# First row stage of a spectral filter and token-mixing kernel: row norms in pairs, the fold ahead of its small copy, a new order of loads and of VectorE and ScalarE

## The chip, the core and the metric

The kernel runs on one core of one Trainium2 chip. The time is the device time of one execution in microseconds (us). Of the kernel before, three executions are at hand besides a profiled one.

A core has TensorE (PE in the profile; its weight loads are PEld), VectorE (DVE), ScalarE (ACT), GpSimd (POOL) and SyncE (SP), which here only issues DMAs. Each engine works through its own instructions in the order in which they were written. What crosses from one engine to another is guarded by semaphores.

## The reference, cut to what matters

```python
def _A_ref(x, w_r, w_i):                       # spectral filter over tokens and channels
    X = jnp.fft.rfft2(x, axes=(-2, -1)) * (w_r + 1j * w_i)
    return jnp.fft.irfft2(X, s=(S, D), axes=(-2, -1))
def _B_ref(x, w1, b1, w2, b2):                 # token-mixing MLP, with its own layernorm
    u = _gelu(jnp.einsum("bsd,sf->bdf", _layernorm(x), w1) + b1)
    return (jnp.einsum("bdf,fs->bds", u, w2) + b2).transpose(0, 2, 1)
x = x + _A_ref(_layernorm(x), A_w_r, A_w_i)
x = x + _B_ref(_layernorm(x), B_w1, B_b1, B_w2, B_b2)
x = x + _A_ref(_layernorm(x), A_w_r, A_w_i)
x = x + _B_ref(_layernorm(x), B_w1, B_b1, B_w2, B_b2)
```

S is 2048, D 640, all in float32. The change concerns the first lines of this: the layernorm of the input x and the first step of the first Fourier transform.

## The kernel before

The 2048 tokens are laid out as 16 tiles of 128 partitions, called rows here (NJ is 16); a row is 128x640. The program is a sequence: the first row stage (in `run`), then for each of two rounds the column stage `a1` (the transforms over tokens, the filter and back), `a2` (back to channels, sum, second layernorm) and the MLP. The second round has its own row stage, which the change leaves as it is but for one load.

The first row stage takes each row i through these steps, each named here as its output is named in the profile:

- SP loads the row (`xt`) and, one per turn, a slab of the filter (`w`); at turns 4, 8 and 12 a quarter of the table of cosines and sines (`tM`), which serves four rows. Quarter 0 is loaded at the start, between row 1 and row 2.
- VectorE takes the row's statistics: two instructions for the halves (`st`, `stats1`), their aggregate (`mv`, `stats2`), and variance plus epsilon (`v`).
- GpSimd raises `v` to the power -0.5 (`r`; `mh` holds -0.5) and makes the offset `nb`, minus mean times r.
- ScalarE writes the normalized row (`z`), alternately into two buffers.
- GpSimd folds z (`eo`): two instructions on 128x320 each, the sum and the difference of mirrored halves (`a0_fold0`). VectorE copies two single columns of z into `eo` ahead of that (the small copy); GpSimd's fold waits for it.
- VectorE makes the rest, `fr`: two additions on 128x64 and a copy of two columns (`a0_rest`).
- TensorE multiplies `eo` and `fr` by the table and by its negative, which ScalarE writes (`tM<-tM`), after one filling matmul (`a0_s1f`). A filling matmul multiplies constants (`fill`); 28 stand ahead of row 0.
- ScalarE writes the result in half precision (`s1h`), VectorE what that leaves out (`s1l`).

Beside this ScalarE squares the filter's slabs (`jw`, into `xq`), whose largest sum sets a scale, `sx`. That takes two small products on TensorE with VectorE steps around them (`scale_x`, a generator whose steps are taken one by one): a product of `xq` with a unit matrix `eye`, a maximum (`xm`, `xb`), a product of `xb` with `eye`, then arithmetic on 128x16. `scale_b` does the like for a bias (`bsq`, `sqb`, `qb`).

The order of the work is that of the loop over i in `run`, turns 0 to 20 (NJ + 5): in turn i an engine works on different rows, the statistics of row i, the norm of row i-1, z of row i-2, fold, `fr` and matmuls of row i-3, `s1h` of row i-4, `s1l` of row i-5. Since `self.pin` is set, each engine keeps the order in which the loop writes its instructions.

The column stage follows. Its `dstage(g)` reads `s1h` and `s1l` of all rows at once (the profile's `tD,s1h`); four matmuls on `tD` stand ahead of it to keep TensorE busy. Part of `s1h` and `s1l` goes through memory and back, in another shape (`rest`, `stk`). The order in there is written by hand in `STEPS`: `d1@1` is dstage(1) into PSUM slot 1, `sA0@2` the first half of the next transform, and an entry that starts with e takes a step of one of the scale generators (`scale`: with a number above 7, of `scale_x`).

Buffers that matter: `eo` has three, `fr`, `r`, `nb`, `v`, `mv` and `st` two each, rows of x six, `w` four.

Of the kernel before, what the change touches and what calls it, by code (L numbers as in the profile page):

```python
# [11 lines left out]
F32 = mybir.dt.float32  # L12
# [3 lines left out]
AF = mybir.ActivationFunctionType  # L16
# [12 lines left out]
STEPS = '''  # L29
    d1@1 sA0@2 ph1 pl1 sB0 d2@3 sA1@0 d3@1 ph2&1 tb0 ta0 pl2 sa0 ph3 sB1 sb0 sA2@2 d4@3  # L30
    tb1 xh0&2 pl3 sB2 sA3@1 ta1 ph4&3 tb2 ta2 xl0 d6@0 sa1 sb1 ph6 sB3 xh1 d5@2 pl4 sa2 ta3 pl6 sb2 sA4@3 ph5 tb3 ul0&4
# [61 lines left out]
class Layers:  # L93
# [170 lines left out]
    def scale_x(self, pool, ps):  # L264
# [7 lines left out]
        V.tensor_copy(b, m.to_broadcast([NG, 128]))  # L272
        yield
        mm(ps[:, 1, 322:322 + NG], b, self.eye[:NG, :NG], start=True, stop=True)
        yield
# [74 lines left out]
    def a0_load(self, *parts):  # L350
        A = self.A
        todo = [(self.tD, A["tD"]), (self.tS2, A["tS2"]), (self.tI2, A["tI2"]), (self.tS1, A["tS1"])]
        for k in parts or range(4):
            self.nc.sync.dma_start(*todo[k])
            if parts == (3,):
                self.nc.sync.dma_start(self.tM32, A["tM32"][:, NJ - 1])

# [53 lines left out]
    def a0_fold0(self, z):  # L411

        G, V = self.G, self.V
# [8 lines left out]
    def a0_rest(self, eo):  # L422
# [93 lines left out]
    def a1(self, first):  # L516
# [1509 lines left out]
    def run(self):  # L2026
# [12 lines left out]
        order = list(range(NW, NG)) + list(range(NW))  # L2039
        x, st, eo, fr, pv, rb = ({} for _ in range(6))  # L2040
# [12 lines left out]
        load(0)  # L2053
        load(1)
        table(0)
        load(2)
        self.pin = True
        for i in range(NJ + 5):
            has = [0 <= i - k < NJ for k in range(6)]
            load(i + 3)  # L2060
            if i in (4, 8, 12):
                table(i // 4)
            for _ in range(2 if i == 5 else 1):
                if i >= 2 and order:
                    scans.append(self.scan_x(pw, order.pop(0)))
# [9 lines left out]
            if has[1]:  # L2075
                v, mv = st.pop(i - 1)
                r = self.t(self.pT, [128, 1], F32, "r", 2)
                self.G.tensor_tensor(r, v, self.mh, op=ALU.pow)
                b = self.t(self.pT, [128, 1], F32, "nb", 2)
                self.G.tensor_scalar(b, mv[:, 0:1], r, -1.0, op0=ALU.mult, op1=ALU.mult)  # L2080
                rb[i - 1] = r, b
            if has[2]:
                r, b = rb.pop(i - 2)
                self.T.activation(z[i % 2][:, :D], x.pop(i - 2), AF.Identity, scale=r, bias=b)
            if i % 4 == 2 and i < NJ:
                q = self.tM[i // 4]
                self.T.activation(q[:, 1], q[:, 0], AF.Copy, scale=-1.0)
            for _ in range(2 if i == 7 else 1):
# [4 lines left out]
            if i == 14:  # L2093
                gb = self.scale_b(at=lambda: px[:, 1, 400:401])
            if i in (14, 15):
                next(gb)
            if has[0]:
                s1 = self.stats1(self.pT, x[i])
                mv = self.stats2(self.pT, s1)
                v = self.t(self.pT, [128, 1], F32, "v", 2)  # L2100
                self.V.tensor_scalar(v, mv[:, 1:2], EPS, None, op0=ALU.add)
                st[i] = v, mv
            if i == NJ + 3:
                next(self.gx)
            if has[5]:
                self.a0_s1l(i - 5, pv.pop(i - 5), 1.0)
            if i == NJ + 2:
# [4 lines left out]
            if has[3]:  # L2112
                fr = self.a0_rest(eo[i - 3])
                pv[i - 3] = self.a0_s1f(i - 3, eo.pop(i - 3), fr)
            if i == NJ + 3:
                next(self.gx)
                next(gb)
        next(self.gx)
        next(gb)
# [223 lines left out]
```

## Time and profile before

| | us |
|---|---|
| median of three executions | 949.59 |
| lowest and highest of them | 948.35, 950.39 |
| the profiled execution's own time | 948.38 |
| its span in the trace | 946.6 |
| TensorE busy in the span | 932.1 (98%) |
| VectorE busy | 753.9 (80%) |
| ScalarE busy | 569.0 (60%) |
| GpSimd busy | 296.8 (31%) |

In the first row stage the shares are others. Of 10 us between 20 and 30 us, VectorE is busy 9.27, ScalarE 9.64, GpSimd 9.53 and TensorE 9.33 (its filling matmuls counted).

How to read the rows of a timeline: start in us from the span's start, duration in us, engine, line of the program, operation, output<-input, shapes, count; in square brackets the idle time ahead of it and what ended it. Rows of one kind that follow each other are merged, so the duration of an x2 is that of both. Instructions of one engine overlap a little: from one start to the next is what an instruction costs the queue. Line 85 is a helper through which all engine calls pass, so instructions are told apart by their tiles. A row of waits gives who waited for whom, the time in all, how often, and the longest. A row of groups gives the busy time in us and the mean in ns behind the bar.

### The profile page before, as it was taken

Reading aid. Unit: us, or ns where it says so; the run is one execution under the profiler, and the core shown is the slowest. Engines: PE = TensorE matmul, PEld = TensorE weight load, DVE = VectorE, ACT = ScalarE, POOL = GpSimd, SP = SyncE. Lnnn points to the kernel's source line nnn. Section 1 sums busy time; section 2 is a strip of 40 time slices with the busy share of each in tenths; the row PEclk is TensorE's granted clock in tenths of the full one; section 3 lists DMA queues with packets and bytes.
Section 4 is the critical chain, followed back from the end, with each engine's and each line's share of the span. In section 5 each row is a group of like instructions: output and inputs, shape, how many; then the busy total and the mean of one; then the engine's idle time right before and its main releaser. Section 6 shows DMA issues by size and latency. Waiting matters only on the chain.

```text
span 946.6 us, 22342 instructions
## 1 busy us (share of the span) xinstructions
PE 932.1 (98%) x8996; PEld 685.5 (72%) x8996; DVE 753.9 (80%) x1411; ACT 569.0 (60%) x861; POOL 296.8 (31%) x453
## 2 busy tenths in 40 slices
PE   8999999999999999999999999999999999999998
PEld 5677777767777777777777777777777777777776
DVE  6869999999788978777775898889745446998885
ACT  5948789885676755555552576783433335465542
POOL 6949688111111033322223695770000000000000
PEclk9999999999999999999999999999999999999999
DMA  8945367555776856855342746774455446665411
GB/s 282 323 127 172 117 225 237 204 178 204 289 265 234 292 179 220 281 177 173 118 136 81 204 137 204 256 238 160 157 159 167 142 126 239 198 190 183 137 55 49
DMA packets 68816, 177.84 MB, mean 188 GB/s; under 512 B 7756, under 2 KB 16232, under 8 KB 68712
## 3 DMA queue, kind: packets, MB, share of 16 engines
q1 hardware_dynamic: 62040, 152.30, 49.6%
q0 software_dynamic: 6672, 24.12, 6.7%
q8 instruction: 70, 1.15, 0.5%
q14 instruction: 34, 0.28, 0.1%
HBM read 128.81 MB, written 47.58 MB: 186 GB/s over the span
## 4 chain that ended last, share of the span: by engine, by line
PE 81%; DVE 9%; POOL 3%; ACT 3%; DMA 2%; issue 2%; SPq 0%; DVEq 0%; ACTq 0%; POOLq 0%
PE ps L85 81%; DVE st L85 2%; DMA xt<-x 1%; POOL xl L85 1%; DVE s1l L85 1%; DMA raw<-w 1%; POOL ta L85 1%; DVE xt L85 1%; POOL eo L85 1%; DVE hl L85 1%; DVE hf L85 1%; DVE hlb L85 1%; DVE fr L85 1%; POOL xt L85 0%; ACT eh L85 0%
## 5 line engine op out<-in xcount | busy, mean ns | idle before, releaser
L85 PEld LDWEIGHTS <-wh 128*128 128x128 f16 x2290 | 221.9, 98 | 85.9 <-ACT wh L85 0.4
L85 PE MATMUL ps<-u,wh 128*128 128x320 f16 x1234 | 227.2, 299 | 0.0
L85 PEld LDWEIGHTS <-wl 128*128 128x128 f16 x1617 | 157.8, 98 | 62.5 <-issue 1.2
L85 PE MATMUL ps<-u,wl 128*128 128x320 f16 x817 | 180.7, 299 | 0.0
L85 PEld LDWEIGHTS <-wo 128*128 128x128 f16 x917 | 89.6, 98 | 34.8
L85 POOL TENSOR_TENSOR r<-v,mh 128x1 f32<-128x1 f32 x64 | 38.2, 596 | 119.7 <-DVE nm L85 113.0
L85 PE MATMUL ps<-tDi,Yh 128*128 128x322 f16 x320 | 70.0, 300 | 0.9 <-ACT Yh L85 0.8
L85 ACT ACTIVATE junk<-raw 128x896 bf16<-128x896 f32 (+1 forms) x60 | 59.5, 992 | 10.3 <-DMA raw<-w 9.6
L85 DVE SCALAR_TENSOR_TENSOR wl<-raw,s,wh 128x896 f16<-128x896 f32 (+2 forms) x43 | 56.3, 1317 | 11.3 <-ACT wh L85 11.3
L85 POOL TENSOR_TENSOR eo<-z 128x320 f32<-128x320 f32 x60 | 57.8, 983 | 21.4 <-ACT z L85 14.8
L85 POOL TENSOR_TENSOR xt<-xt,ec 128x320 f32<-128x320 f32 x64 | 53.2, 853 | 29.2 <-DVE xt L85 29.1
L85 DVE BATCH_NORM_STATS2 st<-xt 128x6 f32<-128x320 f32 x126 | 55.5, 482 | 4.9 <-DMA xt<-x 4.1
L85 PE MATMUL ps<-u,wo 128*128 128x320 f16 x413 | 57.9, 299 | 0.0
L85 PE MATMUL ps<-tDi,Yl 128*128 128x322 f16 x192 | 54.2, 299 | 0.1
L85 ACT ACTIVATE wh<-raw,s 128x896 f16<-128x896 f32 (+2 forms) x46 | 45.1, 988 | 6.5 <-PE ps L85 6.5
L85 POOL TENSOR_TENSOR xl<-ta,xh 128x642 f16<-128x642 f32 (+2 forms) x34 | 45.7, 1347 | 4.7 <-ACT xh L85 4.5
L85 DVE SCALAR_TENSOR_TENSOR u<-f,su,u 128x1280 f16<-128x1280 f32 (+2 forms) x26 | 25.5, 997 | 25.2 <-ACT u L85 25.1
L85 PE MATMUL ps<-hhb,wh 128*128 128x320 f16 x256 | 43.4, 299 | 0.0
L85 ACT ACTIVATE z<-xt,nb,r 128x640 f32<-128x640 f32 x31 | 28.5, 918 | 24.0 <-POOL z L85 15.7
L85 PE MATMUL ps<-tD,s1h 128*64 128x160 f16 (+1 forms) x576 | 39.2, 236 | 0.8 <-ACT s1h L85 0.5
L85 PEld LDWEIGHTS <-Yh 128*128 128x128 f16 x320 | 28.7, 97 | 14.4 <-ACT Yh L85 1.2
L85 DVE SCALAR_TENSOR_TENSOR f<-ps,cp,f 128x320 f32<-128x320 f32 x41 | 22.4, 545 | 19.7 <-PE ps L85 19.7
(267 smaller groups left out, 2199.0 us busy)
## 6 DMA issues: line engine op xcount, KB each, us to landing
xt<-x SPq DMA_DIRECT2D x79, 320.0 KB, 3.0
raw<-w SPq DMA_DIRECT2D x32, 512.0 KB, 7.1
x<-xt SPq DMA_DIRECT2D x47, 320.0 KB, 2.8
raw<-w SPq DMA_DIRECT2D x32, 448.0 KB, 4.9
raw<-w2z SPq DMA_DIRECT2D x32, 448.0 KB, 4.0
w<-w SPq DMA_DIRECT2D x43, 321.0 KB, 4.6
out<-xt SPq DMA_DIRECT2D x15, 320.0 KB, 2.2
w1S<-wl POOLq DMA_DIRECT2D x9, 512.0 KB, 6.6
```

The costliest lines, as they stand in the source:

```text
L85: i = f(*a, **k)
```

## The change

1. *Norms in pairs.* Rows 0 and 1 keep a norm each. From row 2 on two rows share one: the aggregates go side by side into one tile, `v` and a new tile `nm` (minus the mean, on VectorE) are made for both rows by one instruction each in the turn of the second row, and GpSimd makes `r` and `nb` on 128x2. `nb` is now a product of two tensors, `nm` and `r`. These norms are taken in even turns, for rows i-2 and i-1, and stand on GpSimd ahead of the fold of row i-3.
2. *The small copy behind the fold.* The copy of two columns moves from `a0_fold0` to the head of `a0_rest`, behind the fold in the program's order; GpSimd's fold no longer waits for it.
3. *Loads.* Row 2 is loaded ahead of table quarter 0. The table in memory is cut into four pieces of 128x512, each contiguous; before, a quarter was 2 KB out of every 8 KB. The second load of slab `w` in turn 5 is gone; one is loaded per turn.
4. *Order.* `fr` and the matmuls of a row move one turn later (row i-4 in turn i), and `s1h` with them (row i-5). `s1h` now stands at the head of ScalarE's turn; z stands ahead of the filter's squaring in odd turns and turns below 5 and behind it in the others. VectorE's turn begins with the small copy and `fr`, then come the statistics, `s1l`, and only then the aggregate, `v` and `nm`. z has three buffers.
5. *Scales.* The product of `xq` with `eye` moves behind the last row's matmuls; that of `xb` into the column stage, ahead of dstage(1) (`ep9`), and the arithmetic on 128x16 behind it (`ev9`). `bsq` is squared in turn 13 instead of 14 and reduced in turn 15.
6. *Filling.* 20 filling matmuls ahead of row 0 instead of 28, and two on `tD` instead of four ahead of dstage(0).

On VectorE, in the middle of the stage, one turn before, from the statistics of row 7:

```order
L85 BN_STATS st_453<-xt_327 128x6 x2
L85 BN_AGGR mv_456<-st_453 128x2
L85 TENSOR_SCALAR v_458<-mv_456 128x1
L85 SCALAR_TENSOR_TENSOR s1l_195<-ps_393,s1h_194 128x160x4
L85 TENSOR_TENSOR fr_461<-eo_441 128x2x32
L85 TENSOR_TENSOR fr_461<-eo_441 128x64
L85 COPY fr_461<-eo_441 128x2
L85 COPY eo_481<-z_218 128x2
```

And now, the odd turn with the statistics of row 7 (`xt_289`), from its head to its end:

```order
L85 COPY eo_381<-z_217 128x2
L85 TENSOR_TENSOR fr_417<-eo_381 128x2x32
L85 TENSOR_TENSOR fr_417<-eo_381 128x64
L85 COPY fr_417<-eo_381 128x2
L85 BN_STATS st_429<-xt_289 128x6 x2
L85 SCALAR_TENSOR_TENSOR s1l_195<-ps_393,s1h_194 128x160x4
L85 BN_AGGR mv_404<-st_429 128x2
L85 TENSOR_SCALAR v_434<-mv_404 128x2
L85 TENSOR_SCALAR nm_436<-mv_404 128x2
```

`fr` has moved ahead of the statistics, `s1l` between the statistics and their aggregate, and `v` and `nm`, for rows 6 and 7 together, stand at the end; the even turn lacks these two.

On GpSimd, some rows in, before (`eo` is a fold, `r` and `nb` a norm):

```order
L85 TENSOR_TENSOR eo_370<-z_217 128x2x160 x2
L85 TENSOR_TENSOR r_374<-v_349,mh 128x1
L85 TENSOR_SCALAR nb_376<-mv_347,r_374 128x1
L85 TENSOR_TENSOR eo_405<-z_218 128x2x160 x2
L85 TENSOR_TENSOR r_409<-v_386,mh 128x1
L85 TENSOR_SCALAR nb_411<-mv_384,r_409 128x1
```

And now:

```order
L85 TENSOR_TENSOR eo_345<-z_219 128x2x160 x2
L85 TENSOR_TENSOR r_377<-v_368,mh 128x2
L85 TENSOR_TENSOR nb_379<-nm_370,r_377 128x2
L85 TENSOR_TENSOR eo_381<-z_217 128x2x160 x2
L85 TENSOR_TENSOR eo_411<-z_218 128x2x160 x2
L85 TENSOR_TENSOR r_447<-v_434,mh 128x2
L85 TENSOR_TENSOR nb_449<-nm_436,r_447 128x2
```

Instead of a norm after each fold there is one norm, twice as wide, after each two. The fold right behind the norm (`eo_381`, row 3) is the one that the odd turn of VectorE shown above begins with.

The diff, cut to its core:

```diff
@@ STEPS
-    d1@1 sA0@2 ph1 pl1 sB0 d2@3 ...
+    ep9 d1@1 ev9 sA0@2 ph1 pl1 sB0 d2@3 ...
@@ scale_x
     yield
+        ps = self.px
         mm(ps[:, 1, 322:322 + NG], b, self.eye[:NG, :NG], start=True, stop=True)
@@ a0_fold0
-        V.tensor_copy(eo[:, 0:162:161], z[:, 0:162:161])
         G.tensor_tensor(v2(eo, 1, 161), za, zb, op=ALU.add)
@@ a0_rest
+        V.tensor_copy(eo[:, 0:162:161], z[:, 0:162:161])
@@ a0_s1f
-        for _ in range(FILL if j else 28):
+        for _ in range(FILL if j else 20):
@@ a1
+        self.px = slots[3]
-            for _ in range(4):
+            for _ in range(2):
@@ run
-        z = [self.pT.tile([128, 642], F32, name=f"z{k}") for k in range(2)]
+        z = [self.pT.tile([128, 642], F32, name=f"z{k}") for k in range(3)]
-            nc.sync.dma_start(self.tM[q][:, 0], A["tM32"][:, 4 * q:4 * q + 4])
+            nc.sync.dma_start(self.tM[q][:, 0], A["tM32"][q].rearrange("p (a b) -> p a b", a=4))
+        def norms(k, n):
+            r = self.t(self.pT, [128, 2], F32, "r", 2)[:, :n]
+            self.G.tensor_tensor(r, vs[k], self.mh[:, 0:1].to_broadcast([128, n]), op=ALU.pow)
+            b = self.t(self.pT, [128, 2], F32, "nb", 2)[:, :n]
+            self.G.tensor_tensor(b, nms[k], r, op=ALU.mult)
+            for q in range(n):
+                rb[k + q] = r[:, q:q + 1], b[:, q:q + 1]
         load(0)
         load(1)
+        load(2)
         table(0)
-        load(2)
-            for _ in range(2 if i == 5 else 1):
-                if i >= 2 and order:
+            if i >= 2 and order:
+            if has[1] and i - 1 in one:
+                norms(i - 1, 1)
+            elif has[1] and i % 2 == 0:
+                norms(i - 2, 2)
             if has[3]:
-                eo[i - 3] = self.a0_fold0(z[(i - 3) % 2])
+                eo[i - 3] = self.a0_fold0(z[(i - 3) % 3])
+            if has[5]:
+                self.a0_s1h(i - 5, pv[i - 5], 1.0)
+            if i % 2 or i < 5:
+                norm()
...
+            if not i % 2 and i > 4:
+                norm()
             if has[4]:
-                self.a0_s1h(i - 4, pv[i - 4], 1.0)
+                fr = self.a0_rest(eo[i - 4], z[(i - 4) % 3])
+                pv[i - 4] = self.a0_s1f(i - 4, eo.pop(i - 4), fr)
             if has[0]:
                 s1 = self.stats1(self.pT, x[i])
-                mv = self.stats2(self.pT, s1)
...
             if has[5]:
                 self.a0_s1l(i - 5, pv.pop(i - 5), 1.0)
+            if has[0]:
+                k, n = (i, 1) if i in one else (i - i % 2, 2)
+                if k == i:
+                    mv = self.t(self.pT, [128, 2, 2], F32, "mv", 2)[:, :n]
+                self.V.bn_aggr(mv[:, i - k], s1)
+                if i - k == n - 1:
+                    vs[k] = self.t(self.pT, [128, 2], F32, "v", 2)[:, :n]
+                    self.V.tensor_scalar(vs[k], mv[:, :, 1], EPS, None, op0=ALU.add)
+                    nms[k] = self.t(self.pT, [128, 2], F32, "nm", 2)[:, :n]
+                    self.V.tensor_scalar(nms[k], mv[:, :, 0], -1.0, None, op0=ALU.mult)
@@ _shape_tables
-    t["tM32"] = (m1 * TS).astype(np.float32)
+    t["tM32"] = (m1 * TS).astype(np.float32).reshape(128, 4, 512).transpose(1, 0, 2)
```

`norm()` writes z of row i-2 and, in turns 3, 6, 10 and 14, the negative of a table quarter.

More of the change, by code (lines that the diff above doesn't have):

```diff
@@ L29 @@
 STEPS = '''
[L30 removed]
+    ep9 d1@1 ev9 sA0@2 ph1 pl1 sB0 d2@3 sA1@0 d3@1 ph2&1 tb0 ta0 pl2 sa0 ph3 sB1 sb0 sA2@2 d4@3
     tb1 xh0&2 pl3 sB2 sA3@1 ta1 ph4&3 tb2 ta2 xl0 d6@0 sa1 sb1 ph6 sB3 xh1 d5@2 pl4 sa2 ta3 pl6 sb2 sA4@3 ph5 tb3 ul0&4
@@ L355, in a0_load @@
             if parts == (3,):
-                self.nc.sync.dma_start(self.tM32, A["tM32"][:, NJ - 1])
+                self.nc.sync.dma_start(self.tM32, A["tM32"][3, :, 384:])
     CA, CB = 1.0 / ZS ** 2, EPS / ZS ** 2
@@ L411, in a0_fold0 @@
     def a0_fold0(self, z):
-        G, V = self.G, self.V
+        G = self.G
         eo = self.t(self.pT, [128, 646], F32, "eo", 3)
@@ L420, in a0_fold0, with a0_rest @@
         return eo
-    def a0_rest(self, eo):
+    def a0_rest(self, eo, z):
         V = self.V
@@ L2039, in run @@
         order = list(range(NW, NG)) + list(range(NW))
-        x, st, eo, fr, pv, rb = ({} for _ in range(6))
-        z = [self.pT.tile([128, 642], F32, name=f"z{k}") for k in range(2)]
+        x, eo, pv, rb, vs, nms = ({} for _ in range(6))
+        z = [self.pT.tile([128, 642], F32, name=f"z{k}") for k in range(3)]
         for q in z:
@@ L2050, in table @@
         def table(q):
-            nc.sync.dma_start(self.tM[q][:, 0], A["tM32"][:, 4 * q:4 * q + 4])
+            nc.sync.dma_start(self.tM[q][:, 0], A["tM32"][q].rearrange("p (a b) -> p a b", a=4))
[6 more added lines that the diff above has]
+                rb[k + q] = r[:, q:q + 1], b[:, q:q + 1]
         load(0)
         load(1)
+        load(2)
         table(0)
-        load(2)
         self.pin = True
+        one = 0, 1
         for i in range(NJ + 5):
@@ L2062, in run @@
                 table(i // 4)
-            for _ in range(2 if i == 5 else 1):
-                if i >= 2 and order:
-                    scans.append(self.scan_x(pw, order.pop(0)))
+            if i >= 2 and order:
+                scans.append(self.scan_x(pw, order.pop(0)))
             if i == 8:
@@ L2072, in run @@
                     self.a0_load()
+            if has[1] and i - 1 in one:
+                norms(i - 1, 1)
+            elif has[1] and i % 2 == 0:
+                norms(i - 2, 2)
             if has[3]:
-                eo[i - 3] = self.a0_fold0(z[(i - 3) % 2])
[L2075 to L2088, printed above, removed]
+                eo[i - 3] = self.a0_fold0(z[(i - 3) % 3])
+            if has[5]:
+                self.a0_s1h(i - 5, pv[i - 5], 1.0)
+            def norm():
+                if has[2]:
+                    r, b = rb.pop(i - 2)
+                    self.T.activation(z[(i - 2) % 3][:, :D], x.pop(i - 2), AF.Identity, scale=r, bias=b)
+                if i in (3, 6, 10, 14):
+                    q = self.tM[i // 4]
+                    self.T.activation(q[:, 1], q[:, 0], AF.Copy, scale=-1.0)
@@ L2089, in run @@
+            if i % 2 or i < 5:
+                norm()
+            for _ in range(2 if i == NJ + 2 else 1):
                 if i >= 4 and scans:
                     scans.pop(0)()
-            if has[4]:
-                self.a0_s1h(i - 4, pv[i - 4], 1.0)
[L2093 to L2096, printed above, removed]
+            if not i % 2 and i > 4:
+                norm()
+            if i == 13:
+                gb = self.scale_b(at=lambda: px[:, 1, 400:401])
@@ L2097, in run @@
+            if i in (13, 15):
+                next(gb)
+            if has[4]:
+                fr = self.a0_rest(eo[i - 4], z[(i - 4) % 3])
+                pv[i - 4] = self.a0_s1f(i - 4, eo.pop(i - 4), fr)
             if has[0]:
                 s1 = self.stats1(self.pT, x[i])
-                mv = self.stats2(self.pT, s1)
-                v = self.t(self.pT, [128, 1], F32, "v", 2)
-                self.V.tensor_scalar(v, mv[:, 1:2], EPS, None, op0=ALU.add)
-                st[i] = v, mv
             if i == NJ + 3:
-                next(self.gx)
@@ L2105, in run @@
-            if has[5]:
-                self.a0_s1l(i - 5, pv.pop(i - 5), 1.0)
-            if i == NJ + 2:
                 assert not scans
@@ L2111, in run @@
                 next(self.gx)
[L2112 to L2115, printed above, removed]
+            if i == NJ + 4:
                 next(self.gx)
                 next(gb)
-        next(self.gx)
+            if has[5]:
+                self.a0_s1l(i - 5, pv.pop(i - 5), 1.0)
+            if has[0]:
[8 more added lines that the diff above has]
+                    self.V.tensor_scalar(nms[k], mv[:, :, 0], -1.0, None, op0=ALU.mult)
         next(gb)
```

## The prediction

> **What bounds the kernel now.** I read the page first, for the span and the engine that carries the end.
>
> ```profile
> span 946.6 us, 22342 instructions
> PE 81%; DVE 9%; POOL 3%; ACT 3%; DMA 2%; issue 2%; SPq 0%; DVEq 0%; ACTq 0%; POOLq 0%
> ```
>
> PE carries four fifths of the chain. The change touches only the first row stage, the first 52 us, so I read that stage alone: its waits, then the timeline of VectorE and GpSimd. The steady part of the stage (14 to 44 us) repeats every 2.56 us. On VectorE one row is:
>
> ```profile
> 25.14 0.88 DVE L85 BATCH_NORM_STATS2 st<-xt 128x6 f32<-128x320 f32 x2
> 26.12 0.21 DVE L85 BATCH_NORM_AGGREGATE mv<-st 128x2 f32<-128x12 f32 x1
> 26.37 0.15 DVE L85 TENSOR_SCALAR v<-mv 128x1 f32<-128x1 f32 x1
> 26.44 0.81 DVE L85 SCALAR_TENSOR_TENSOR s1l<-ps,s1h 128x640 f16<-128x640 f32 x1
> 27.17 0.35 DVE L85 TENSOR_TENSOR fr<-eo 128x64 f32<-128x64 f32 x2
> 27.55 0.17 DVE L85 COPY fr<-eo 128x2 f32<-128x2 f32 x1
> 27.63 0.16 DVE L85 COPY eo<-z 128x2 f32<-128x2 f32 x1
> 27.70 0.88 DVE L85 BATCH_NORM_STATS2 st<-xt 128x6 f32<-128x320 f32 x2
> ```
>
> On GpSimd, the same stretch:
>
> ```profile
> 24.50 0.56 POOL L85 TENSOR_TENSOR r<-v,mh 128x1 f32<-128x1 f32 x1
> 25.15 0.27 POOL L85 TENSOR_SCALAR nb<-mv,r 128x1 f32<-128x1 f32 x1
> 25.38 1.72 POOL L85 TENSOR_TENSOR eo<-z 128x320 f32<-128x320 f32 x2
> 27.06 0.55 POOL L85 TENSOR_TENSOR r<-v,mh 128x1 f32<-128x1 f32 x1
> ```
>
> Each row of either engine starts where the one ahead of it lets go: both are full at 2.56 us (25.14 to 27.70, 24.50 to 27.06). TensorE has slack; in the waits of 14 to 44 us (total, times, longest) it stands for the folds, and VectorE once for ScalarE's bsq:
>
> ```profile
> PEld ps L85 <- POOL eo L85: 5.8, 11, 0.7
> ...
> DVE sqb L85 <- ACT bsq L85: 0.6, 1, 0.6
> ```
>
> So this stage is set by VectorE and GpSimd together, and a row gains only what both give up.
>
> At the head, the first fold waits behind the statistics of row 2, which wait for a DMA:
>
> ```profile
> 3.60 0.89 DVE L85 BATCH_NORM_STATS2 st<-xt 128x6 f32<-128x320 f32 x2 [1.87 <-DMA xt<-x]
> 4.77 0.15 DVE L85 TENSOR_SCALAR v<-mv 128x1 f32<-128x1 f32 x1
> 8.40 0.89 DVE L85 BATCH_NORM_STATS2 st<-xt 128x6 f32<-128x320 f32 x2 [2.26 <-DMA xt<-x]
> 9.71 0.16 DVE L85 COPY eo<-z 128x2 f32<-128x2 f32 x1
> ```
> ```profile
> 5.00 0.55 POOL L85 TENSOR_TENSOR r<-v,mh 128x1 f32<-128x1 f32 x1 [4.14 <-DVE v L85]
> 6.88 0.27 POOL L85 TENSOR_SCALAR nb<-mv,r 128x1 f32<-128x1 f32 x1
> 9.96 1.70 POOL L85 TENSOR_TENSOR eo<-z 128x320 f32<-128x320 f32 x2 [2.81 <-DVE eo L85]
> ```
> ```profile
> 5.95 0.92 ACT L85 ACTIVATE z<-xt,nb,r 128x640 f32<-128x640 f32 x1 [1.02 <-POOL nb L85]
> 7.46 0.63 ACT L85 ACTIVATE tM<-tM 128x512 f32<-128x512 f32 x1 [0.59 <-DMA tM<-tM]
> ```
>
> z of row 0 is done at 6.87 (5.95 + 0.92), the fold starts at 9.96: 3.1 us lie between.
>
> **The change, part by part.** I follow three marks: V5 and V15, the starts of v for rows 5 and 15, and E, the end of row 15's last matmul. Before, V5 is 15.97, V15 42.49, E 52.31 (51.93 + 0.38):
>
> ```profile
> 15.97 0.15 DVE L85 TENSOR_SCALAR v<-mv 128x1 f32<-128x1 f32 x1
> ...
> 42.49 0.15 DVE L85 TENSOR_SCALAR v<-mv 128x1 f32<-128x1 f32 x1
> ```
> ```profile
> 49.97 0.39 PE L85 MATMUL ps<-fill 128*128 128x512 f16 x1
> 50.20 1.89 PE L85 MATMUL ps<-tM,eo 128*128 128x256 f32 x8
> 51.93 0.38 PE L85 MATMUL ps<-tM,fr 128*128 128x128 f32 x2
> 52.24 0.39 PE L85 MATMUL ps<-eye,xb 16*128 16x16 f32 x2
> ...
> 52.60 1.02 PE L85 MATMUL ps<-tD 128*128 128x512 f16 x4
> 53.55 1.33 PE L85 MATMUL ps<-tD,s1h 128*64 128x160 f16 x32
> ```
> ```profile
> 52.35 0.70 ACT L85 ACTIVATE s1h<-ps 128x640 f16<-128x640 f32 x1 [1.90 <-PE ps L85]
> ```
>
> *Head.* x2 now stands ahead of the table in SP's queue. By windows of the DMA view, the stretches 0 to 3.8, 3.8 to 6.4 and 6.4 to 9 us moved:
>
> ```profile
> DMA packets 274, 0.64 MB, mean 169 GB/s; under 512 B 22, under 2 KB 22, under 8 KB 274
> DMA packets 192, 0.37 MB, mean 142 GB/s; under 512 B 25, under 2 KB 25, under 8 KB 192
> DMA packets 462, 1.05 MB, mean 404 GB/s; under 512 B 50, under 2 KB 50, under 8 KB 462
> ```
>
> The first 0.64 MB are x0 and x1 (0.33 each); then 2.6 us at 142 GB/s, just until the table lands (7.46, about 1 us behind its bytes); then full speed. I take the slow stretch to be the table, 2 KB pieces out of rows of 8 KB. x2 then follows x1 at full speed: bytes done at 4.6, landed at 5.6 instead of 8.4. If the table, now contiguous, runs at 400 GB/s too, x3 lands at 7.1; if it stays slow, at 9.0. Now by hand: nb of row 1 ends near 7.14 (before 6.88 + 0.27; one more VectorE instruction per row, 0.07, and a shorter nb on GpSimd), and the fold of row 0, which no longer waits for VectorE, runs 7.15 to 8.85. Rows 2 and 3 share one norm, which needs both: statistics at 6.22 and 7.45, v at 8.68, pow at 8.9. Then nb, and the fold of row 1 ends at 11.4 + d, where d is what a second column adds to pow. V5 follows 2.27 later (below): 13.7 + d. Gain 2.3 - d.
>
> *Two rows at a time.* Throughput alone would promise much: GpSimd loses half of 0.91 per row, and VectorE, with s1l between the statistics and their aggregate, loses the wait of 0.18 (0.98 to 0.80) and some of v: 2.56 to about 2.4. But the order makes a loop. GpSimd does the norm for rows i-2, i-1 ahead of the fold of row i-3; VectorE's next odd turn begins with the rest of that same row (its copy, fr), and its v comes at that turn's end. The loop is one for two rows: v to pow 0.23 (4.77 to 5.00), pow to nb 0.65 + d (24.50 to 25.15), nb 0.17, folds 1.68 (25.38 to 27.06), to fr 0.03 (a bare hand-over), fr and copy 0.47, statistics 0.80, s1l 0.73, aggregate to v 0.24. Sum 5.00 + d, against 5.12. nb is now a product of two tensors, as in the later rows:
>
> ```profile
> L85 POOL TENSOR_TENSOR nb<-nm,r 128x1 f32<-128x1 f32 x15 | 2.8, 189 | 1.2
> ```
>
> From its 0.189 to pow's 0.55 there are 0.36; if that is all per column, d is 0.36, if none, 0. I take the middle, 0.18, since no row has pow on two columns. Below 0 it can't be: two columns hold the work of one. The Trainium skill (GPSIMD Engine Reference, section 3.1) gives about 2.6 cycles per element for an ordinary two-input operation; by that d is about 0.002 us and the sum would be 4.4 rather than 3.2, but no run here shows that it holds for pow. Five loops, V5 to V15: 25.0 + 5d against 26.52 (which holds 0.6 of waiting for ScalarE's bsq, now issued two turns earlier). Gain 1.5 - 5d. The small copy now also stands behind a fold: hidden under the fold's second half if it waits for the first only; if for both, 0.08 per loop, 0.4 in all. I take it as hidden.
>
> *Tail.* Rows 12 to 15 end on TensorE. A row there takes 2.3 us: fill 0.23 (49.97 to 50.20), eo 1.73 to 1.83, fr 0.27. Row 12's start waits for its small copy (V15 + 0.25), row 13 ends near V15 + 4.8, row 15 at V15 + 9.4 + d/2, against 9.82 before. Gain 0.4 - d/2.
>
> *Behind E.* Before, E to the first s1h matmul is 1.24. Two warming matmuls fewer save 0.5 of it, but s1h of row 15 (0.70 on ScalarE) ends no earlier, so the first matmul starts at E + 0.85 or so. The xq product now stands behind E, under that wait; the xb product (about 0.2) moves behind the first s1h group, so 0.2 of the 0.35 is paid back: gain 0.2, bounds 0 and 0.4. The chain sx (four VectorE instructions) moves too, into VectorE's idle time there. Eight fills fewer cost nothing, since they only cover the wait for row 0. The third z buffer and its 0.1 us MEMSET lie in GpSimd's idle head.
>
> Sum: 2.3 - d + 1.5 - 5d + 0.4 - d/2 + 0.2 = 4.4 - 6.5d, at d = 0.18: 3.2 us. The profiled execution took 948.38 (span 946.6 and 1.8 around it) and would take 945.2; it is the fastest of three whose median is 949.59, so the median should go to 946.4. Behind E the order of work is the same but for the sx steps, so I expect the shift to arrive in full. The measurement can tell about 0.2%, 1.9 us.
>
> **Rivals.**
>
> 1. *The table stays slow* (the slow stretch is not its row pitch). x3 lands at 9.0, v of row 3 is at 10.27, V5 at 15.3 + d: head gain 0.7 - d, sum 2.8 - 6.5d = 1.6: 948.0. For it: no row says that the pitch is the cause; the first touch of a tensor could be slow too. Against it: x0, the first touch of its tensor, ran in the faster stretch.
>
> 2. *The two-row loop costs more than it saves: slower.* Place: norm, fold, fr, statistics, v, once in two rows. If pow on two columns costs two whole instructions (d = 0.55), the small copy waits for the whole fold (0.4), and the table stays slow, the sum is 2.8 - 3.6 - 0.4 = -1.2: 950.8. With the copy's 0.4 it turns negative from d = 0.37 on, or from 0.62 if the table is fast. For it: pow is the dearest one-column step of the stage (0.55 against 0.15 for v), and pairing puts the second row's norm ahead of an earlier row's fold. Against: the fixed cost is visible in nb's 0.189 for one column.
>
> 3. *TensorE's clock drops at the head.* Two queries of TensorE's timeline, to 9 and to 13 us, group the fills:
>
> ```profile
> 1.79 7.54 PE L85 MATMUL ps<-fill 128*128 128x512 f16 x22 [1.79 <-DVE fill L2034]
> ...
> 1.79 8.83 PE L85 MATMUL ps<-fill 128*128 128x512 f16 x28 [1.79 <-DVE fill L2034]
> ```
>
> The last six took 1.29, 0.215 each; for 22 to take 7.54, some 12 at the start took twice that, until about 7 us. Twenty fills end near 8.9; if row 0 starts at 10.5 (rival 1), TensorE idles 1.6 us. If that brings the early rate back for as long as it held at first (1.79 to 7, 5.2 us), half of that, 2.6, is lost: gain 0.6, 949.0. The trace holds no such gap behind the fills, so nothing in it speaks for the drop. The Trainium skill (TensorE: Matmul & The Clock Gate, Part 1) says that the clock halves after an idle window of about 3.4 us and comes back after a busy one; the trace agrees on the two rates, not on the time, and by that rule 1.6 us would not suffice.
>
> 4. *The gain is lost behind E*: the next stage waits for the transfers of s1h and s1l through memory or for VectorE, whatever E does. Then nothing arrives: 949.6. Against: those transfers start from row 15's s1l too.
>
> **How the numbers follow.** Forecast (table fast, d between 0 and 0.36) 0.52; rival 1 0.28; rival 2 0.09; rival 3 0.05; rival 4 0.06. The forecast's own gains run from 2.1 (d = 0.36) to 4.4, rival 1's from 0.5 to 2.8. The range goes from a gain of 4.4 and the executions' scatter of about 1 (944.2) to rival 1's worst with the copy in line and a little scatter (949.8). Faster by over 1.9 us: nine tenths of the forecast (0.47), two fifths of rival 1 (0.11), a little of rival 3 (0.02): 0.60. Slower: rival 2, whose worst lies beyond 1.1 only if scatter helps, taken whole as a caution, with what I overlook: 0.09. Within: 0.31.
>
> **What would show it.** In the profile after: the fold of row 0 starts near 7.15; statistics of row 2 near 6.2 and of row 3 near 7.5 (rival 1: 9.0); r on 128x2 lasts 0.73 (0.55 to 0.91); two rows take about 5.16 us, with VectorE waiting about 0.5 before each second fr for GpSimd's eo, and GpSimd about 0.5 for v; E near 49.2. The prediction is wrong if two rows take under 4.8 (the loop isn't there) or over 5.3, if x2 still lands near 8, or if E moves and the end doesn't.

## The result and the profile after

| | before | after |
|---|---|---|
| median, four executions each (us) | 949.08 | 956.08 |
| lowest and highest | 948.35, 950.39 | 955.30, 958.46 |
| the profiled execution's own time | 948.38 | 955.76 |
| its span | 946.6 | 954.0 |

After to before is 1.0082, with a 95% interval of 1.007 to 1.0094: slower by 7 us, where 3 us of gain were forecast. The time lies above the range, which ended at 949.8.

On the page of after, TensorE's share of the chain has gone from 81% to 80% and VectorE's from 9% to 11%:

```profile
PE 80%; DVE 11%; ACT 3%; issue 2%; DMA 2%; POOL 2%; SPq 0%; ACTq 0%; DVEq 0%; POOLq 0%
```

Nearly all of it, 6.8 of the 7.4 us by which the span grew, arises in the first row stage. The waits of after between 14 and 44 us (total, times, longest) show who stands there now:

```profile
POOL r L85 <- DVE nm L85: 11.0, 5, 2.2
PEld ps L85 <- DVE eo L85: 10.6, 9, 1.7
PE ps L85 <- DVE eo L85: 7.1, 9, 1.3
```

GpSimd, full before, now waits 2.2 us in every two rows for `nm`, and TensorE for VectorE's part of `eo`. The timeline of GpSimd in after, over two rows (x4 is two folds, one right behind the other):

```profile
15.87 0.76 POOL L85 TENSOR_TENSOR r<-v,mh 128x2 f32<-128x2 f32 x1 [2.20 <-DVE nm L85]
...
16.85 3.34 POOL L85 TENSOR_TENSOR eo<-z 128x320 f32<-128x320 f32 x4
22.39 0.74 POOL L85 TENSOR_TENSOR r<-v,mh 128x2 f32<-128x2 f32 x1 [2.20 <-DVE nm L85]
```

And that of VectorE in the same two rows:

```profile
15.77 0.16 DVE L85 COPY eo<-z 128x2 f32<-128x2 f32 x1
15.84 0.35 DVE L85 TENSOR_TENSOR fr<-eo 128x64 f32<-128x64 f32 x2
...
17.93 0.63 DVE L85 COPY eo<-z 128x2 f32<-128x2 f32 x1
18.58 1.70 DVE L85 TENSOR_TENSOR fr<-eo 128x64 f32<-128x64 f32 x2
```

Two rows take 6.52 us (15.87 to 22.39) and not 5.16. The same two `fr` instructions last 0.35 at 15.84, beside the norm, and 1.70 at 18.58, beside the second fold; the small copy 0.16 and 0.63. They are not shown as waiting: they have started and do not end. The second `fr` ends at 20.28, just behind the second fold (16.85 + 3.34 = 20.19). The difference of 1.35 (1.70 - 0.35) is the whole of what a pair lasts too long.

The head went as forecast, in the rows of VectorE and then of GpSimd:

```profile
6.31 0.88 DVE L85 BATCH_NORM_STATS2 st<-xt 128x6 f32<-128x320 f32 x2
...
7.86 0.89 DVE L85 BATCH_NORM_STATS2 st<-xt 128x6 f32<-128x320 f32 x2 [0.43 <-DMA xt<-x]
```
```profile
7.18 1.70 POOL L85 TENSOR_TENSOR eo<-z 128x320 f32<-128x320 f32 x2
9.35 0.75 POOL L85 TENSOR_TENSOR r<-v,mh 128x2 f32<-128x2 f32 x1 [0.47 <-DVE nm L85]
```

And the end of the stage on TensorE:

```profile
58.76 0.38 PE L85 MATMUL ps<-tM,fr 128*128 128x128 f32 x2
...
59.84 0.16 PE L85 MATMUL ps<-sqb,ones 128*128 128x1 bf16 x1 [0.37 <-DVE xm L85]
...
60.38 1.33 PE L85 MATMUL ps<-tD,s1h 128*64 128x160 f16 x32
```

E is 59.14 (58.76 + 0.38), 6.83 later than before. TensorE itself was not slowed: the eight `eo` matmuls of row 0 last 1.99 us, as before, and the mean granted clock is 0.999.

### The profile page after: what moved, and what is told of

It is laid out like the page before. It is cut to its first block, busy times and chain, and to the rows that moved or that the text cites. A ratio compares the mean times of both kernels' runs of the same rounds, so it can differ in the third digit from the quotient of the medians.

```text
span 954.0 us, 22301 instructions
## 1 busy us (share of the span) xinstructions
PE 930.7 (98%) x8986; PEld 684.8 (72%) x8986; DVE 767.1 (80%) x1413; ACT 570.1 (60%) x861; POOL 292.8 (31%) x440
## 4 chain that ended last, share of the span: by engine, by line
PE 80%; DVE 11%; ACT 3%; issue 2%; DMA 2%; POOL 2%; SPq 0%; ACTq 0%; DVEq 0%; POOLq 0%
PE ps L85 80%; DVE fr L85 2%; DVE st L85 1%; DVE s1l L85 1%; DVE Yl L85 1%; DMA raw<-w 1%; DVE xt L85 1%; DVE eo L85 1%; ACT eh L85 1%; DVE hl L85 1%; DVE hf L85 1%; DVE hlb L85 1%; DMA xt<-x 1%; DVE ta L85 1%; DVE tb L85 1%
## 5 line engine op out<-in xcount | busy, mean ns | idle before, releaser
L85 POOL TENSOR_TENSOR r<-v,mh 128x1 f32<-128x1 f32 (+1 forms) x57 | 35.8, 628 | 133.5 <-DVE nm L85 131.2
L85 PE MATMUL ps<-tM,eo 128*128 128x256 f32 x128 | 31.8, 391 | 9.9 <-DVE eo L85 9.8
L85 ACT ACTIVATE s1h<-ps 128x640 f16<-128x640 f32 (+2 forms) x33 | 22.5, 685 | 31.2 <-PE ps L85 31.0
```

The lines of the kernel that those rows point to most:

```text
L85: i = f(*a, **k)
```

## The experiments

The theory, T1: some VectorE instructions, `fr` (two inputs in SBUF) and the small copy among them, cannot run while a fold runs on GpSimd. Pairing the norms put two folds behind one another, so that one `fr` in two always falls under a fold, and that `fr` lies on the loop of the two rows. The rivals are other reasons for the long loop: the pairing itself (R2), the copy's new place (R3), the loads (R1), and other forms of the hold (R4, R5). All times below are compared with the kernel before on the same chip, whose medians there were 947.98 (first four), 948.41 (next four) and 948.65 (last two).

**The loads alone.** In the kernel before:

```diff
         load(0)
         load(1)
+        load(2)
         table(0)
-        load(2)
...
-        nc.sync.dma_start(self.tM[q][:, 0], A["tM32"][:, 4 * q:4 * q + 4])
+        nc.sync.dma_start(self.tM[q][:, 0], A["tM32"][q].rearrange("p (a b) -> p a b", a=4))
...
```

The table is laid out in memory to match.

> The kernel before with only the two load edits: the third x row issued ahead of the table piece, and the table stored in four contiguous pieces. Theory T1 (the new slowness lies in VectorE's two-input instructions held by GpSimd's second fold, and only there): these edits do only good, the fold of row 0 starts 2.0 to 2.8 us earlier than the 9.96 of before, the two-row loop stays at 5.1 to 5.2 us, the end of row 15's last matmul comes 2 to 2.8 us earlier, 946 to 947.5 us, faster than before. Rival R1 (the loads of the new order themselves, competing with x rows later on, cost time in the loop): two rows take over 5.4 us here as well, and the time is that of before or slower.

946.21, ratio 0.9975 (0.9963 to 0.9987): faster. The fold of row 0 starts at 7.88 instead of 9.96, the end of row 15 comes at 50.27 (49.89 + 0.38) instead of 52.31, 2.0 earlier, and the rows follow each other at 2.56 us as before. R1 falls; this part of the change is good by itself.

**One wait more.** In the changed kernel the second fold of a pair waits for the `fr` ahead of it (`fr` is therefore written ahead of the fold; the engines' own orders stay but for one reduction of `bsq` on VectorE):

```diff
-        G.tensor_tensor(v2(eo, 1, 161), za, zb, op=ALU.add)
+        first = G.tensor_tensor(v2(eo, 1, 161), za, zb, op=ALU.add)
+        if after is not None:
+            self.tc.add_manual_dep(first.ins, after.ins.name, ...)
...
-        V.tensor_tensor(f4[:, 1:3], ea, eb, op=ALU.subtract)
+        self.lastfr = V.tensor_tensor(f4[:, 1:3], ea, eb, op=ALU.subtract)
...
-                eo[i - 3] = self.a0_fold0(z[(i - 3) % 3])
+                eo[i - 3] = self.a0_fold0(z[(i - 3) % 3], self.lastfr if has[4] and i % 2 else None)
```

> The changed kernel with one wait added: in each odd turn GpSimd's fold starts only after VectorE's second fr subtraction of the row folded before it, so no fr lies under a fold. T1: the copy falls to 0.16 to 0.2 us and the two fr together from 1.70 to 0.7 or less, GpSimd stands idle about 1 us for it, two rows take 5.3 to 5.9 us against 6.52, and the time falls from 956.1 to 948.5 to 952: a wait more makes it faster. Rival R2 (the pairing of the norms lengthens the loop by itself, since the second row's fold and fr now stand between one nm and the next; the long fr only fills a wait): two rows stay at 6.4 or more and the time is 955.5 to 962.

946.8, ratio 0.9983 (0.9972 to 0.9994): 1.2 us under the kernel before, where the changed kernel is 7 above it. A wait that GpSimd did not have gains 8 us, a little more than T1 gave. On GpSimd and on VectorE:

```profile
14.26 0.76 POOL L85 TENSOR_TENSOR r<-v,mh 128x2 f32<-128x2 f32 x1 [0.27 <-DVE nm L85]
...
15.24 1.69 POOL L85 TENSOR_TENSOR eo<-z 128x320 f32<-128x320 f32 x2
17.50 1.69 POOL L85 TENSOR_TENSOR eo<-z 128x320 f32<-128x320 f32 x2 [0.56 <-ACT s1h L85]
19.43 0.74 POOL L85 TENSOR_TENSOR r<-v,mh 128x2 f32<-128x2 f32 x1 [0.25 <-DVE nm L85]
```
```profile
16.33 0.63 DVE L85 COPY eo<-z 128x2 f32<-128x2 f32 x1
16.97 0.36 DVE L85 TENSOR_TENSOR fr<-eo 128x64 f32<-128x64 f32 x2
```

GpSimd gives 0.56 us between the folds, and `fr` lasts 0.36 in that gap. (The row names ScalarE's `s1h`, which ends at 17.42. But the fold starts 0.14 to 0.18 behind the `fr` subtraction in every pair, here behind 17.33, and in the first pair, at 12.29, before `s1h` has ended at 12.37: the wait is for `fr`.) Two rows take 5.17 us, less than T1's 5.3 to 5.9, since GpSimd stands idle 0.56 and not 1. The copy is still held, which T1 did not expect, and costs nothing, since the `fr` behind it needs the first fold anyway. R2 falls: with the pairs kept, only the place of `fr` was changed.

**The copy ahead of the fold again.** One line back from `a0_rest` to `a0_fold0`:

```diff
         eo = self.t(self.pT, [128, 646], F32, "eo", 3)
+        self.V.tensor_copy(eo[:, 0:162:161], z[:, 0:162:161])
...
-        V.tensor_copy(eo[:, 0:162:161], z[:, 0:162:161])
```

> The changed kernel with VectorE's 2-column copy back ahead of the fold, where it stood before. T1: the fr still lies under the second fold and ends with it, so two rows take 6.2 to 6.6 us and the time is 953.5 to 957. Rival R3 (the copy behind the fold is what is late: it takes 0.6 to 0.8 us and pushes the fr into the fold): the fr gets ahead of the fold, two rows fall to 5.5 or less, 948 to 950.

950.36, ratio 1.0025 (1.0012 to 1.0038), and two rows take 5.73 (16.25 to 21.98): between the two expectations, and T1 was wrong on what this edit does.

```profile
18.32 0.63 DVE L85 COPY eo<-z 128x2 f32<-128x2 f32 x1
18.95 0.36 DVE L85 TENSOR_TENSOR fr<-eo 128x64 f32<-128x64 f32 x2
```
```profile
17.23 1.69 POOL L85 TENSOR_TENSOR eo<-z 128x320 f32<-128x320 f32 x2
19.09 1.77 POOL L85 TENSOR_TENSOR eo<-z 128x320 f32<-128x320 f32 x2 [0.17 <-DVE eo L85]
```

The second fold now has to wait for its own copy, which is held under the first fold until 18.95. In the 0.17 us until the fold starts, `fr` slips in ahead of it (18.95 against 19.09). So the old order of copy and fold works as a gate of the same kind as the wait above, by chance and with another copy held: the last one of the rest, 0.72 at 19.35. R3 is right that `fr` gets ahead of the fold here. That the copy's lateness is the cost, it has wrong: with the added wait the copy is held just as long, 0.63, and two rows take 5.17. This part of the change, which I had costed at nothing (or 0.4), is what exposed `fr` to the second fold: with it undone the kernel is 2.4 us above the kernel before, and not 7.

**Norms one by one.** All else as changed:

```diff
-        one = 0, 1
+        one = range(NJ)
```

> The changed kernel with the norms' powers one row at a time throughout (a pow and a product for each row instead of one for two), all else as changed. T1: between any two folds stands a norm of 0.75 us, the fr runs beside it at 0.35 for each instruction, a row takes 2.4 to 2.6 us and the time is 944.5 to 948, under both kernels. If the copy (0.16) pushes the second fr past the norm into the next fold, the second fr is held, a row takes 2.9 or more and the time is 952 or more. Rival R2 (it is the pairing and not the place of the fr): also 945 to 948, but with the fr at any length; T1 and R2 are told apart by the fr rows of this run and by the run with the added wait.

947.34, ratio 0.9987 (0.9974 to 0.9999). A norm stands between any two folds, and `fr` falls beside it:

```profile
17.70 0.55 POOL L85 TENSOR_TENSOR r<-v,mh 128x1 f32<-128x1 f32 x1
...
18.46 1.70 POOL L85 TENSOR_TENSOR eo<-z 128x320 f32<-128x320 f32 x2
20.29 0.55 POOL L85 TENSOR_TENSOR r<-v,mh 128x1 f32<-128x1 f32 x1
```
```profile
17.76 0.36 DVE L85 TENSOR_TENSOR fr<-eo 128x64 f32<-128x64 f32 x2
```

Two rows take 5.02 (15.27 to 20.29), less than either kernel. Doing without the pairs is faster than the pairs with the wait in the loop, but the head is later here (the fold of row 0 starts at 8.62, behind the norm of row 2).

**Kinds of instruction, by themselves.** This kernel leaves out the layers, so only durations are read from it. Three of each of ten kinds run on VectorE, alone and beside a chain on GpSimd:

```diff
+        for k, (n, g) in enumerate(chains):
...
+            for q in range(n):
+                g(q % 2)
...
+            for f in kinds:
+                for q in range(N):
+                    f(q)
```

> The layers are left out: this kernel only loads one row block and runs ten kinds of VectorE instruction, three of each in a row, first with GpSimd idle and then beside a chain of GpSimd instructions, once of the fold's kind (TENSOR_TENSOR 128x320, two inputs in SBUF), once of the pow (TENSOR_TENSOR 128x2), once of one input (TENSOR_SCALAR 128x320); its time has no meaning and only durations are read. T1: beside the fold's kind the instructions with two SBUF inputs (add 128x64, SCALAR_TENSOR_TENSOR 128x640 from SBUF) and the copies of SBUF to SBUF last until the GpSimd instruction under way ends, about 0.85 us each, and the same with an input in PSUM, BN_STATS and TENSOR_SCALAR keep the duration that they have alone within a tenth; beside the pow nothing changes. Rival R4 (simple sharing of the bandwidth): every SBUF kind grows by a like factor of less than 2, BN_STATS too, and the small ones hardly.

First the rows with GpSimd idle, then the same beside the fold's kind (`tt` adds 128x64 from SBUF, `ttp` the same with one input in PSUM; `cp` and `ts` are three of 128x2 and three of 128x64; `stt` has two inputs in SBUF, `stp` one in PSUM):

```profile
5.67 0.50 DVE L25 TENSOR_TENSOR tt<-z,y 128x64 f32<-128x64 f32 x3
6.08 0.48 DVE L25 TENSOR_TENSOR ttp<-ps,y 128x64 f32<-128x64 f32 x3
6.47 0.60 DVE L25 COPY cp<-z 128x2 f32<-128x2 f32 x6
6.98 0.61 DVE L25 TENSOR_SCALAR ts<-z 128x2 f32<-128x2 f32 x6
...
9.08 2.29 DVE L25 SCALAR_TENSOR_TENSOR stt<-z,y 128x640 f16<-128x640 f32 x3
...
15.49 1.82 DVE L25 TENSOR_TENSOR tt<-z,y 128x64 f32<-128x64 f32 x3
17.24 0.47 DVE L25 TENSOR_TENSOR ttp<-ps,y 128x64 f32<-128x64 f32 x3
17.64 2.23 DVE L25 COPY cp<-z 128x2 f32<-128x2 f32 x6
19.78 2.60 DVE L25 TENSOR_SCALAR ts<-z 128x2 f32<-128x2 f32 x6
...
22.69 1.27 DVE L25 BATCH_NORM_STATS2 bst<-z 128x6 f32<-128x320 f32 x3
23.88 3.60 DVE L25 SCALAR_TENSOR_TENSOR stt<-z,y 128x640 f16<-128x640 f32 x3
27.41 2.27 DVE L25 SCALAR_TENSOR_TENSOR stp<-ps,y 128x640 f16<-128x640 f32 x3
```

Two inputs in SBUF are held (0.50 to 1.82, 2.29 to 3.60), copies from SBUF to SBUF too (0.60 to 2.23), and what has an input in PSUM, or is BN_STATS, is not touched: 1.27 here, 1.28 alone. So R4, by which every kind from SBUF would stretch by a like factor, BN_STATS too, falls. T1 missed TENSOR_SCALAR from SBUF: it is held like the copy (0.61 to 2.60). And 0.85 for each add was too much: the first falls at the end of an instruction of the chain, and the three take 1.82. Beside the chain of pows `tt` lasts 0.49 and `cp` 0.60: a pow holds nothing that can be seen.

**`fr` under the fold without pairs.** In the version with single norms:

```diff
+            if has[0]:
+                s1 = self.stats1(self.pT, x[i])
             if has[4]:
                 fr = self.a0_rest(eo[i - 4], z[(i - 4) % 3])
                 pv[i - 4] = self.a0_s1f(i - 4, eo.pop(i - 4), fr)
-            if has[0]:
-                s1 = self.stats1(self.pT, x[i])
```

> The version with single norms, and in it VectorE's rest of a row (copy, two fr instructions, copy) stands behind the statistics of the next row instead of ahead of them; nothing else differs. T1: the rest then begins 0.9 us later, when GpSimd has gone over from the norm to the next fold, so the copy and the first fr are held for an instruction of the fold each; the rest takes 1.7 us and more instead of 0.9, a row 3.2 to 3.6 us instead of 2.5, and the time is 956 to 964. Rival R2 (it is the pairing that made the loop long, not where the fr lies): without pairs the order of these VectorE instructions is worth at most 0.2 us a row, 944 to 950.

950.5, ratio 1.0024 (1.0014 to 1.0034): 3.5 us more, by the ratios, than the version that it alters, but not the 9 and more that T1 gave. The two engines drift against each other. Until 20 us `fr` still falls beside the norms and a row takes 2.42 (17.90 to 20.32); then VectorE's turn slides into the fold:

```profile
20.78 0.36 DVE L85 TENSOR_TENSOR fr<-eo 128x64 f32<-128x64 f32 x2
21.17 0.86 DVE L85 COPY fr<-eo 128x2 f32<-128x2 f32 x1
```
```profile
20.32 0.54 POOL L85 TENSOR_TENSOR r<-v,mh 128x1 f32<-128x1 f32 x1
...
23.20 0.55 POOL L85 TENSOR_TENSOR r<-v,mh 128x1 f32<-128x1 f32 x1 [0.37 <-DVE nm L85]
...
26.79 0.46 POOL L85 TENSOR_TENSOR nb<-nm,r 128x1 f32<-128x1 f32 x1
```

From there rows take 2.4 to 3.7. Mostly it is the last copy of the rest, and not `fr`, that is held (0.86 instead of 0.17). The time lies 0.5 above R2's range and 5.5 below T1's, so it speaks against T1's size more than against R2. What speaks against R2 is the rows: without any pair, the order on VectorE alone brings the hold, and rows up to 1.3 us longer.

**The fold first, once.** In the version with single norms:

```diff
+            if i == 3:
+                eo[0] = self.a0_fold0(z[0])
             if has[1] and i - 1 in one:
                 norms(i - 1, 1)
...
-            if has[3]:
+            if has[3] and i > 3:
                 eo[i - 3] = self.a0_fold0(z[(i - 3) % 3])
```

> The version with single norms, with one exchange: in the fourth turn GpSimd runs the fold of row 0 ahead of the norm of row 2. T1 with the head as forecast: fold of row 0 starts near 7.1 instead of 8.62, TensorE's first real matmul near 9.2 instead of 10.4, and, as VectorE sets the pace of 2.5 us a row behind that, the end comes 0.5 to 1.2 us earlier: 945.5 to 947, faster than before. Rival: VectorE's own chain (the third and fourth rows' statistics) sets the start of the loop, and nothing changes, 947 to 948.

945.57, ratio 0.9968 (0.9957 to 0.9978): the lowest ratio here, though its interval overlaps that of the loads alone (0.9963 to 0.9987). The fold of row 0 starts at 7.14; TensorE's first real matmul comes at 9.55, a little later than expected, and E is 49.22 (48.84 + 0.38).

**Fewer fillings.** On top of the loads alone:

```diff
-        for _ in range(FILL if j else 28):
+        for _ in range(FILL if j else 20):
```

> The kernel before with the two load edits, and 20 filling matmuls ahead of row 0 instead of 28. In the run of the load edits alone TensorE began row 0 at 10.21, straight behind its fillings, while the fold of row 0 had ended at 9.55: the fillings had become the wait. T1 for the head: row 0 starts near 9.7, but two rows still take 5.1 us by the loop over GpSimd and VectorE, so the end comes 0 to 0.5 us earlier, 945.7 to 946.7. Rival (the fillings hold TensorE's clock): the granted clock falls below 1.0 in the first 20 us and the time is that of the load edits plus 0.5 to 3.

947.13, ratio 0.9989 (0.9978 to 0.9999). Row 0 on TensorE starts at 8.80 instead of 10.21, earlier than the 9.7 expected, and the column stage is reached no earlier (GpSimd's first step there starts at 58.81 in both). Nothing is gained: the loop sets the end. The median is 0.9 above that of the loads alone and so in the rival's range, not in T1's; the intervals do not separate the two runs. The rival's reason is not there: the granted clock stays at 1.0, and E is 50.28 against 50.27. What lies behind the stage stays open.

**The fold in halves.** In the changed kernel each fold instruction is cut in two:

```diff
-        G.tensor_tensor(v2(eo, 1, 161), za, zb, op=ALU.add)
-        self.lastpool = G.tensor_tensor(v2(eo, 322, 161), za, zb, op=ALU.subtract)
+        for o, op in (1, ALU.add), (322, ALU.subtract):
+            e = v2(eo, o, 161)
+            for a in range(2):
+                self.lastpool = G.tensor_tensor(e[:, a], za[:, a], zb[:, a], op=op)
```

> The changed kernel with each of GpSimd's two fold instructions (128x320) cut into two of 128x160; nothing else differs, and a fr still lies under the second fold. T1 in its sharp form (a VectorE instruction that finds the fold running waits for the end of the GpSimd instruction under way, no longer): the pieces last about 0.45 us, so the two fr fall from 1.70 to 0.9 to 1.1 us and the copy ahead of them to 0.45 or less, two rows take 5.4 to 5.9 us instead of 6.52, and the time is 948 to 952 although GpSimd has twice the instructions. Rival R5 (VectorE gets in only when GpSimd's whole chain of folds is through): the fr last 1.7 us or more as before, two rows 6.5 to 6.9, 955 to 959.

953.77, ratio 1.0058 (1.0038 to 1.0079). The hold follows the length of GpSimd's instruction, as T1 said:

```profile
17.59 0.43 DVE L85 COPY eo<-z 128x2 f32<-128x2 f32 x1
18.52 1.01 DVE L85 TENSOR_TENSOR fr<-eo 128x64 f32<-128x64 f32 x2 [0.49 <-POOL eo L85]
19.57 0.40 DVE L85 COPY fr<-eo 128x2 f32<-128x2 f32 x1
```
```profile
16.51 3.92 POOL L85 TENSOR_TENSOR eo<-z 128x160 f32<-128x160 f32 x8
```

`fr` falls from 1.70 to 1.01: two pieces instead of two instructions. R5 falls. But of these 0.69 us little is left. A piece lasts 0.49 (3.92 / 8), more than half of 0.84 (3.34 / 4), so the fold that `fr` waits for takes about 0.28 longer; and the last copy of the rest is now held too, 0.40 instead of 0.17. Two rows still take 6.34 (15.53 to 21.87), 0.18 less than in the changed kernel. T1's time for this run was too low for these two reasons.

**The old loads in the changed kernel.**

```diff
         load(0)
         load(1)
-        load(2)
         table(0)
+        load(2)
...
-            nc.sync.dma_start(self.tM[q][:, 0], A["tM32"][q].rearrange("p (a b) -> p a b", a=4))
+            nc.sync.dma_start(self.tM[q][:, 0], A["tM32"][:, 4 * q:4 * q + 4])
```

> The changed kernel with the loads as they were: table quarter 0 ahead of the third row, and the table in rows of 8 KB. T1 (the head's gain is real and is there in the changed kernel too, only drowned by the loop): the third row's statistics start near 8.4 instead of 6.3, the first pow for two rows near 11.5 instead of 9.35, and the time rises by 2.0 to 2.6 us over the changed kernel, 957 to 959.5. Rival R6 (in the changed kernel the long loop swallows the head's gain): within 0.7 us of the changed kernel, 954.5 to 956.8.

957.43, ratio 1.009 (1.0076 to 1.0104). The interval overlaps that of the changed kernel, so the times do not decide. The traces do: the first pow for two rows starts at 10.56 instead of 9.35, and row 15 ends at 60.31 (59.93 + 0.38) instead of 59.14, 1.2 later. That lies between T1 (2.0 to 2.6) and R6 (0.7). The fold of row 0 starts early here too (7.11), since it does not wait for the copy; in the changed kernel the loads serve only the norm of rows 2 and 3.

## Why the prediction was wrong, point by point

**Failed: "to fr 0.03 (a bare hand-over), fr and copy 0.47".** This term of the loop took the 0.35 that `fr` lasted before, where it lay beside the pow. I did not ask what it would lie beside afterwards. The order had the answer: with the norm taken once in two rows, the fold of one row follows right on the fold whose `fr` is due. Under a fold it lasts 1.70. The run with the added wait shows that this, and only this, is what the loop's term lacked. There the marks are V5 14.01, V15 39.91, E 50.08:

```profile
14.01 0.17 DVE L85 TENSOR_SCALAR v<-mv 128x2 f32<-128x2 f32 x1
...
39.91 0.17 DVE L85 TENSOR_SCALAR v<-mv 128x2 f32<-128x2 f32 x1
```

The forecast had V5 at 13.9 and five loops of 25.9; these are 25.90. In the changed kernel V5 is 15.62 and V15 48.47: five loops of 32.85, 6.3 us longer than before.

**Right: d.** pow on two columns lasts 0.75, so d is 0.20 (forecast 0.18). That the size fits so well is luck: 0.18 was the middle between two bounds.

**Right: the head.** The fold of row 0 starts at 7.18 (forecast 7.15), the statistics of rows 2 and 3 at 6.31 and 7.86 (6.2 and 7.5; rival 1 had 9.0, and falls). V5 at 14.01 in the run with the wait is a gain of 1.96, where 2.1 was forecast. With the loads alone V5 comes at 13.92, 2.05 earlier: up to V5 the rest of the change adds nothing to them. In the stretch from 3.8 to 6.4 us the DMA moved 142 GB/s before and 321 after. Order and layout of the loads were changed together in every run, so which of the two does it is not shown.

**Wrong side: rival 2.** The slower rival had the right place, the two-row loop, and wrong prices: a dear pow and a late copy, 950.8 at worst. No rival had the hold.

**Mis-sized: the tail.** E - V15 is 10.67, 0.85 more than before instead of 0.3 less: `fr` is held there as well (1.70 at 51.42).

**Wrong: behind E.** From E to the first `s1h` matmul it is 1.24 (59.14 to 60.38), as before, so the 0.2 is not gained: `ones` stands behind `xq` and waits 0.37 for `xm`. And the `xb` product, now inside dstage(1), costs 0.43. In the run with the added wait, between `s1l` and the next `s1h`:

```profile
52.48 0.72 PE L85 MATMUL ps<-tD,s1l 128*64 128x160 f16 x16
53.14 0.39 PE L85 MATMUL ps<-eye,xb 16*128 16x16 f32 x2
53.46 0.33 PE L85 MATMUL ps<-tD,s1h 128*64 128x160 f16 x4
```

0.98 (52.48 to 53.46), and with the loads alone, where `xb` lies ahead of the stage, 0.55:

```profile
52.69 0.72 PE L85 MATMUL ps<-tD,s1l 128*64 128x160 f16 x16
53.24 0.31 PE L85 MATMUL ps<-tD,s1h 128*64 128x160 f16 x4
```

The sum for the changed kernel: V5 0.35 earlier, five loops 6.33 later, tail 0.85 later: E 6.83 later, then 0.43 for `xb`: 7.3 of the 7.4 by which the span grew.

**Rivals 3 and 4.** Rival 3 falls by TensorE's own rows: with single norms TensorE waited 1.95 us for row 0, and the eight `eo` matmuls behind that wait took 1.99, as they did before behind a wait of 0.26. (The granted clock can't decide it: it reads 1.00 before in the first 4 us too, where six fills take 2.74 and not the 1.29 of the last six.) Rival 4 falls as well: what E loses arrives in full, and so does what it gains; with the loads alone E is 2.0 earlier, GpSimd's first step of the column stage 2.0 (58.81 instead of 60.84), and the median 1.8 lower.

## What to carry to other kernels

When an order moves, look at what each instruction will lie beside, not only at what it waits for: a duration read from a trace holds for the neighbour that it had there. VectorE's copies, TENSOR_SCALARs and two-input instructions on SBUF are best placed beside a GpSimd instruction that holds nothing (here the pow) or in a gap left for them; a wait that makes such a gap can shorten the loop, as 0.56 us of idle GpSimd did here by 1.35. A step that separates two long GpSimd instructions may be worth keeping even where merging it saves work.

## What the runs showed of the hardware that was not expected

- A VectorE instruction with both inputs in SBUF, or a copy or TENSOR_SCALAR from SBUF to SBUF, that finds an instruction of the fold running on GpSimd is not done before that ends: three adds of 0.50 take 1.82 beside a chain of them, and the two `fr` 1.70 beside fold instructions of 0.84 and 1.01 beside pieces of 0.49. It is shown as busy, not as waiting. The Trainium skill (SBUF — State Buffer, section "Who interferes with whom") says this: VectorE's second pair of ports is GpSimd's only one, whoever starts first has it for the whole instruction, and it lists these kinds. For the fold the traces agree on the kinds and on the length of the hold; the prediction had not weighed that.
- A pow of 0.74 us on GpSimd, which reads SBUF too, holds nothing that can be seen: three adds beside it take 0.49. By the rule of the Trainium skill in the same section, for a GpSimd instruction that reads SBUF, it should; the measurement decides.
- The hold goes the other way too. An add of the chain on GpSimd, 0.86 alone, lasts 1.53 where an `stt` starts beside it (23.87 and 23.88), and `nb` 0.46 instead of 0.19 where `fr` does (26.79 and 26.85, `fr` under the fold without pairs).
- GpSimd with one input (TENSOR_SCALAR 128x320, 1.005 us each) holds less than the fold: beside it the six copies take 0.89, three `stt` 2.85 and three adds 0.48.
